# A linear-attention and bilinear-GLU block on one core: the last seven block products, six of them turned so that the weights stand still

## The chip, the cores and the metric

The kernel runs on one core of one Trainium2 chip. The core has a matrix engine (TensorE, PE in the profile), three engines for elementwise work (VectorE or DVE, ScalarE or ACT, GpSimd or POOL) and SyncE (SP), which here issues every transfer between the chip's memory (DRAM) and the on-chip buffers. A matmul holds one 128-wide operand still in the array (it is loaded first, "PEld" in the profile) and streams the other through it, up to 512 columns at a time, and adds the result into a bank of the accumulator memory (PSUM). The metric is the device time of one execution in microseconds (us), and a kernel's time is the median of its runs.

## What is computed

The reference is one transformer block with modulated layer norms: linear attention, then a bilinear gated feed-forward part. Only the second half matters here:

```python
h = _layernorm(x, axis=-1) * (1 + cb) + sb
# _B_ref:
g = jnp.einsum("bsd,df->bsf", x, w_gate)
u = jnp.einsum("bsd,df->bsf", x, w_up)
h = g * u
return jnp.einsum("bsf,fd->bsd", h, w_down)
# and the end:
x = x + gb * _B_ref(h, B_w_gate, B_w_up, B_w_down)
```

There are S = 2048 tokens, D = 512 model columns and F = 1376 hidden columns, all in 32-bit floats. The stage that is changed is the last einsum for the second 1024 tokens, and the addition to x behind it.

## The kernel before

**Numbers.** Every 32-bit matrix is split into a high and a low part (ACT rounds the high part, DVE or POOL subtracts it to get the low one), and a product of two matrices is three matmuls: high by high, high by low, low by high. The helper `split` (L198 to L200) and `h_split`, `h_next`, `w_split` of the class `Down` do this; their outputs are called kh and kl for the hidden values, w for the weights.

**Tokens and columns.** The tokens stand in four chunks of 512 (`NCH` = 4, `CH` = 512), a chunk in four tiles of 128 tokens by 512 columns (`xts[ch][j]`, j = 0 to 3). Token p*4 + j of a chunk stands in partition p of tile j (views `xv` and `ov`, L53). The hidden columns stand in eleven tiles of 128, the last with 96.

**Gate and up.** For two chunks at a time these products are done as 2x2 blocks with seven block products in place of eight (sums and differences of blocks are formed first; s1 to s4 on the left, t1 to t4 on the right). `block` (L1180) is one hidden tile's pass of seven products of 6 matmuls with 512 tokens moving; it has named points (p1, p5, p6, p2, p7, p3, p4) behind its products, at which other work is handed in. The table `plan`, filled by `Down.planned` (L1485) and by a literal at the end of the kernel, says what happens at which point of which block; this sets the order of each engine's work. All instructions of an engine run in the written order. All transfers stand in one queue on SP, and one that has to wait holds those behind it.

**Down.** For chunks 0 and 1 plain products (`down_group`, L1237) run between the blocks. For chunks 2 and 3 the class `Down` (L1352) again uses seven block products. With c0 = chunk 2 and c1 = chunk 3, `a11` and `a12` are chunk 2's hidden values of the first and second tile of a pair, `a21` and `a22` those of chunk 3; `b11`, `b12`, `b21`, `b22` are the two row tiles of w_down by its two halves of 256 columns (`HALF`). There are five pairs, and one odd tile of 96 rows. While the last blocks run, the weight sums are formed, split, stored to DRAM (`w_park`) and fetched back (`w_fetch`, L1399) shortly before their product.

**The last stage.** `Down.run` (L1519) starts when the last block is done. Its products, in order: p1 = a11 b11, p2 = a12 b21, p3 = s2 t2, p4 = s1 t1, p5 = s3 t3, p6 = s4 b22, p7 = a22 t4; p2, p5, p6 and p7 also carry the odd tile. Before, in all of them the hidden values of one 128-token tile stand still and the weights move. p1, p3, p5 and p7 use `mm` (L1452): 256 weight columns move, three matmuls for each pair and token tile, four token tiles in two banks (`C`, the first two of `others`). p1, p3, p5, p7 add up in the same banks, and after each of them DVE adds what stands there to the part of x to which it belongs. p2, p4 and p6 use `mm_wide` (L1462): high and low weights move together as 512 columns, then the low hidden values with 256; they have four banks of their own (`A`, the list `banks`). The function `add` (L1525) adds a bank's part to a half of x's columns and stores the tile when it is complete. So each part of x stays in place as tokens by columns, and only 12 stores leave, eight of 128 KB and four of 256 KB. The last product is done tile by tile, in the order 0, 2, 1, 3, each tile's addition and store behind it.

Of the kernel before, what the change touches and what calls it, by code (L numbers as in the profile page):

```python
# [8 lines left out]
F32 = mybir.dt.float32  # L9
# [5 lines left out]
P = 128  # L15
NB = 94
BL = 32
# [7 lines left out]
def tile_adaln_block(  # L25
# [27 lines left out]
    xv = x[0].rearrange("(c p j) d -> c j p d", p=P, j=NJ)  # L53
    ov = out[0].rearrange("(c p j) d -> c j p d", p=P, j=NJ)
# [61 lines left out]
    def load_x(ch):  # L116
        return [load(xv[ch, j], "x") for j in range(NJ)]
# [827 lines left out]
    def evac(ch, dn, js=range(NJ), last=False, cols=((0, D),)):  # L945
        for j in js:
            xt = xts[ch][j]
            for a, b in cols:
                nc.vector.tensor_tensor(xt[:, a:b], dn[j][:, a:b], xt[:, a:b], op=ALU.add)  # L949
                if last:  # L950
                    nc.sync.dma_start(ov[ch, j, :, a:b], xt[:, a:b])
# [342 lines left out]
    banks, others = [], []  # L1294
# [18 lines left out]
    def ffn():  # L1313

        m = 0
        for g, (cs, fs) in enumerate(groups):
# [19 lines left out]
        wide_down = Down((2, 3), m, draws.pop(m))  # L1336
        wide_down.planned()
# [14 lines left out]
    class Down:  # L1352

        def __init__(self, cs, m, odd):
            self.cs, self.m, self.odd = cs, m, odd
# [4 lines left out]
            self.raw, self.t = {}, {}  # L1360

        def w_split(self, key, src, low=None):
            n = src.shape[0]
            w = B("w", (P, 2, HALF), F32R)[:n]
            nc.scalar.activation(w[:, 0], src, AF.Copy)
            (low or nc.vector).tensor_tensor(w[:, 1], src, f32(w[:, 0]), op=ALU.subtract)
            self.w[key] = w

# [93 lines left out]
        def mm_wide(self, bs, j, pairs, start):  # L1462

            a, b = j * P, (j + 1) * P
            for (h, l), w in pairs:
                k = h.shape[0]
                nc.tensor.matmul(bs[j], h[:, a:b], w[:k].rearrange("p t c -> p (t c)"), start=start, stop=False, skip_group_check=True)  # L1467
                nc.tensor.matmul(bs[j][:, :HALF], l[:, a:b], w[:k, 0], start=False, stop=False, skip_group_check=True)
                start = False

        def product(self, bs, js, left, right, start, odd=None):
            pairs = [(self.parts[i][left, "split"], self.w[right, i]) for i in range(self.NI)]
            if odd:
                pairs.append((self.h[LATE[0]][odd[0]], self.w["odd", odd[1]]))
            for j in js:
                if len(bs) == NJ:
                    self.mm_wide(bs, j, pairs, start)
                else:
                    self.mm(bs, j, pairs, start and j % 2 == 0)
# [5 lines left out]
        def planned(self):  # L1485
# [3 lines left out]

            put(1, "p6", lambda: nc.vector.tensor_tensor(self.odd, self.odd, gb[:self.odd.shape[0]], op=ALU.mult))  # L1490
# [27 lines left out]

        def run(self):  # L1519

            c0, c1 = self.cs
            x = lambda c, half, j: xts[c][j][:, half * HALF:(half + 1) * HALF]
            A, C = banks, others[:2]

            def add(c, half, bs, js, store=None):  # L1525
                for j in js:
                    parts = [bs[j][:, :HALF], bs[j][:, HALF:]] if bs is A else [self.part(bs, j)]
                    for ps in parts:
                        nc.vector.tensor_tensor(x(c, half, j), x(c, half, j), ps, op=ALU.add)
                    if store:  # L1530
                        a, b = store
                        nc.sync.dma_start(ov[c, j, :, a:b], xts[c][j][:, a:b])

            lo, hi, js = (0, 1), (2, 3), range(NJ)
            pairs = range(self.NI)
            last = self.NI - 1
# [4 lines left out]
            self.product(C, js, "a11", "b11", True)  # L1541
            self.drop("a11", "b11")
            self.h_next("s2", 0, 1)
            add(c0, 0, C, js)
            self.w_fetch("t1")
            self.product(A, js, "a12", "b21", True, (0, 0))
            self.drop("a12", "b21")
            self.h_next("s2", 2, 3, 4)
            add(c0, 0, A, js)
            self.w_fetch("t3")  # L1550
            self.product(C, js, "s2", "t2", False)
            self.drop("s2", "t2")
            self.h_split("s1", *pairs)
            add(c0, 1, C, js)
            self.w_fetch("b22")
            self.product(A, js, "s1", "t1", True)
            self.drop("s1", "t1")
            self.h_split("s3", *pairs)
            self.h_next("s4", 0)
            add(c1, 1, A, js)  # L1560
            self.w_fetch("t4")
            self.product(C, js, "s3", "t3", False, (1, 1))
            self.drop("s3", "t3")
            self.h_next("s4", 1, 2, 3, 4)
            add(c1, 1, C, js, (HALF, D))
            self.product(A, js, "s4", "b22", False, (0, 1))
            self.drop("s4", "b22")
            self.h_split("a22", *pairs)
            add(c0, 1, A, js, (0, D))
            before = []  # L1570
            for j in (0, 2, 1, 3):
                self.product(C, (j,), "a22", "t4", False, (1, "turn"))
                add(c1, 0, C, before, (0, HALF))
                before = (j,)
            add(c1, 0, C, before, (0, HALF))
# [266 lines left out]
```

## Time and profile before

| | us |
|---|---|
| median of three runs (lowest, highest) | 539.75 (539.24, 540.11) |
| the profiled execution | 539.46 |
| its span, first to last instruction | 537.7 |
| matrix engine busy in the span | 531.5 |
| last stage, first product to the end of the last | 478.46 to 534.05 |
| store queue's last issue starts | 534.50 |

The page of a profile gives for each engine the busy time and its share of the span, and the chain of work that ended last, followed back from the last instruction to what released it. Rows of the chain and of the timeline begin with the start and the length in us; then come the engine, the line of the kernel, the operation, the names of the tiles (written tile, arrow, read tiles), the shape and the count; a bracket at the end gives the idle time before it and what ended it. "SPq" is the transfer queue of SP: its length is what an issue takes on SP, not the transfer itself. Rows of one line's instructions give shortest, median and longest duration in ns. Grouped lines end in total busy us, mean ns of one, and idle time before.

### The profile page before, as it was taken

The page shows a single profiled execution, that of the slowest core. Times are in us where ns is not written, and L with a number is a line of the kernel's source. Part 1 is how long each engine was busy: PE and PEld are TensorE (multiplying, and loading weights), DVE is VectorE, ACT ScalarE, POOL GpSimd, SP SyncE. Part 2 cuts the span into 40 slices and gives each one's busy share as a digit, 9 for nine tenths or more (in the row PEclk, how much of TensorE's full clock was granted, in tenths as well). Part 3 has the DMA queues.
Part 4 walks back from the last instruction along what each step waited for, and adds up shares of the span by engine and source line. Part 5 has one row for each costly group of instructions (what it writes and reads, how often), then busy time and mean ns, then how long its engine had stood idle before and what let it go on. Part 6 is the DMA issues. An engine that isn't in the chain of part 4 may idle for free.

```text
span 537.7 us, 8020 instructions
## 1 busy us (share of the span) xinstructions
PE 531.5 (99%) x2537; PEld 443.4 (82%) x2537; DVE 406.7 (76%) x698; ACT 301.9 (56%) x572; POOL 159.0 (30%) x169
## 2 busy tenths in 40 slices
PE   8999999999999999999999999999999999999997
PEld 6888888888788878878888888887888888889996
DVE  7997879999989888769765576996555564669771
ACT  3696878768587765577684545454434334246030
POOL 2001010000021220085796577747532313210000
PEclk9999999999999999999999999999999999999999
DMA  8912426320165165856869595794289998789122
GB/s 276 385 43 92 144 99 214 86 72 2 45 196 199 36 213 161 280 159 222 290 196 322 196 335 206 232 374 109 81 295 341 395 394 294 237 301 389 53 79 79
DMA packets 86682, 109.21 MB, mean 203 GB/s; under 512 B 11184, under 2 KB 41904, under 8 KB 86640
## 3 DMA queue, kind: packets, MB, share of 16 engines
q1 hardware_dynamic: 86640, 108.70, 60.0%
q8 instruction: 20, 0.33, 0.3%
q14 instruction: 22, 0.18, 0.1%
HBM read 65.93 MB, written 42.73 MB: 202 GB/s over the span
## 4 chain that ended last, share of the span: by engine, by line
PE 93%; DVE 4%; ACT 2%; issue 1%; ACTq 0%; DVEq 0%
PE bank L1162 27%; PE acc L879 8%; PE acc L1162 7%; PE acc L1459 6%; PE bank L214 3%; PE bank L212 3%; PE bank L213 3%; PE bank L1467 3%; PE acc L1246 3%; PE acc L1245 3%; PE acc L1247 3%; PE acc L421 2%; PE acc L420 2%; PE acc L419 2%; PE bank L962 2%; PE bank L964 2%
## 5 line engine op out<-in xcount | busy, mean ns | idle before, releaser
L1162 PE MATMUL bank<-h,w 128*128 128x512 f32 (+1 forms) x630 | 145.3, 389 | 0.0
L1162 PEld LDWEIGHTS bank<-h,w 128*128 128x128 f32 (+1 forms) x630 | 117.0, 186 | 25.9
L1167 ACT ACTIVATE bank<-bank 128x512 f32<-128x512 f32 (+1 forms) x30 | 17.5, 584 | 74.5 <-PE bank L1162 74.4
L200 DVE TENSOR_TENSOR kl<-u,kh 128x512 fp32r<-128x512 f32 (+1 forms) x38 | 26.8, 752 | 23.8 <-ACT kh L199 21.8
L268 POOL TENSOR_TENSOR rstd<-ve,half 128x2 f32<-128x2 f32 (+3 forms) x13 | 11.8, 910 | 107.7 <-DVE ve L267 64.3
L212 PE MATMUL bank<-w,h 128*128 128x512 f32 x104 | 40.6, 391 | 0.0
L214 PE MATMUL bank<-w,h 128*128 128x512 f32 x104 | 40.6, 390 | 0.0
L213 PE MATMUL bank<-w,h 128*128 128x512 f32 x104 | 40.5, 390 | 0.0
L1162 PE MATMUL acc<-h,w 128*128 128x512 f32 x168 | 38.7, 389 | 0.0
L200 POOL TENSOR_TENSOR w<-raw,w 128x512 fp32r<-128x512 f32 (+1 forms) x15 | 22.3, 1496 | 51.7 <-ACT w L199 46.5
L879 PE MATMUL acc<-w,xh 128*128 128x512 f32 x120 | 37.1, 390 | 0.5 <-ACT acc L870 0.5
L1162 PEld LDWEIGHTS acc<-h,w 128*128 128x128 f32 x168 | 31.5, 188 | 6.5
L1124 POOL TENSOR_TENSOR w<-raw,w 128x256 fp32r<-128x256 f32 (+3 forms) x22 | 24.4, 1107 | 37.6 <-ACT w L1117 33.4
L949 DVE TENSOR_TENSOR x<-acc,x 128x512 f32<-128x512 f32 x40 | 26.5, 686 | 11.5 <-PE acc L1247 11.0
L1459 PE MATMUL acc<-w,kh 128*128 128x256 f32 (+1 forms) x176 | 31.8, 283 | 0.0
L1124 POOL TENSOR_TENSOR w<-t,w 128x512 fp32r<-128x512 f32 (+1 forms) x22 | 29.7, 1352 | 0.0
L1459 PEld LDWEIGHTS acc<-w,kh 128*128 128x128 f32 (+1 forms) x176 | 27.5, 192 | 0.2
L879 PEld LDWEIGHTS acc<-w,xh 128*128 128x128 f32 x120 | 22.4, 188 | 5.4 <-ACT acc L870 0.8
L419 PE MATMUL acc<-kh,xh 128*128 128x512 f32 x64 | 25.1, 392 | 0.0
L421 PE MATMUL acc<-kl,xh 128*128 128x512 f32 x64 | 25.0, 390 | 0.0
L420 PE MATMUL acc<-kh,xl 128*128 128x512 f32 x64 | 24.9, 390 | 0.0
L1245 PE MATMUL acc<-w,kh 128*128 128x512 f32 x64 | 24.9, 389 | 0.0
(257 smaller groups left out, 1325.1 us busy)
## 6 DMA issues: line engine op xcount, KB each, us to landing
right<-w SPq DMA_DIRECT2D x56, 256.0 KB, 3.6
w<-right SPq DMA_DIRECT2D x56, 256.0 KB, 5.1
raw<-in_w_mod_dram SPq DMA_DIRECT2D x24, 256.0 KB, 4.3
raw<-in_B_w_down_dram SPq DMA_DIRECT2D x20, 256.0 KB, 4.1
down_t<-w SPq DMA_DIRECT2D x20, 256.0 KB, 5.1
w<-down_t SPq DMA_DIRECT2D x20, 256.0 KB, 5.4
x<-in_A_x_dram SPq DMA_DIRECT2D x16, 256.0 KB, 5.4
down_b<-w SPq DMA_DIRECT2D x15, 256.0 KB, 5.1
```

The lines of the kernel that those rows point to most:

```text
L200: (low or nc.vector).tensor_tensor(l, src, f32(h), op=ALU.subtract)
L212: nc.tensor.matmul(ps, ah, bh, start=i == 0, stop=False)
L213: nc.tensor.matmul(ps, ah, bl, start=False, stop=False)
L214: nc.tensor.matmul(ps, al, bh, start=False, stop=i == n - 1)
L419: nc.tensor.matmul(tacc[k], xh[:, a:b], kh, start=first, stop=False)
L420: nc.tensor.matmul(tacc[k], xl[:, a:b], kh, start=False, stop=False)
L421: nc.tensor.matmul(tacc[k], xh[:, a:b], kl, start=False, stop=last)
L879: nc.tensor.matmul(yps[i], x, y, start=False, stop=k == KD - 1 and x is al, skip_group_check=True)
L1124: sub = lambda out, x, y: (on or nc.gpsimd).tensor_tensor(out, x, f32(y), op=ALU.subtract)
L1162: mm = lambda x, y, **kw: nc.tensor.matmul(ps, x[:, k], y, skip_group_check=True, **kw)
L1245: nc.tensor.matmul(ps, hh[:, a:b], dh[:n, c:d], start=i == 0, stop=False)
L1459: nc.tensor.matmul(ps, x[:, a:b], y, start=start, stop=False, skip_group_check=True)
```

## The change

Six of the seven products are turned: 128 weight columns stand still and the 512 tokens of a whole chunk move. `turned` replaces `mm_wide`:

```diff
+        def turned(self, bank, left, right, fresh, odd=None):
+
+            for m in range(2):
+                ps, start = sets[m][bank], fresh
+                for (h, l), w in self.pairs(left, right, odd):
+                    k = h.shape[0]
+                    of = w[:k, :, m * P:(m + 1) * P]
+                    for x, y in ((0, h), (0, l), (1, h)):
+                        nc.tensor.matmul(ps, of[:, x], y, start=start, stop=False, skip_group_check=True)
+                        start = False
+            self.drop(left, right)
```

The 256 columns of a half go in two sets of 128: set 0 has the even columns, set 1 the odd ones. So that each set is contiguous, `w_split` writes the split weights in that order (all but t4 and the odd tile's difference, which p7 uses as before):

```diff
+            if key[0] != "t4" and key[1] != "turn":
+                src = src.rearrange("p (r m) -> p m r", m=2)
+                h, l = (x.rearrange("p (m r) -> p m r", m=2) for x in (h, l))
+            nc.scalar.activation(h, src, AF.Copy)
+            (low or nc.vector).tensor_tensor(l, src, f32(h), op=ALU.subtract)
```

All eight banks are used, four for each set (`sets`). Bank a holds p1 and then also p2; after p1 ACT copies a to b, to which p3 is added; after p3 ACT copies b to c, to which p5 is added; d holds p4, then p6 is added. So the result of these products stands as columns by tokens. It is copied to the on-chip buffers and brought back in 32x32 blocks by DVE (`flip`), which leaves blocks of 32 tokens by 64 columns; x is read a second time from a copy in DRAM in the same blocks (`x_rows`, written by `x_store` during four of the blocks, read by `x_blocks`), DVE adds it (`finish`), and the blocks go to the output as runs of 64 floats (`move`, four transfers of 64 KB for each tile of 128x512):

```diff
+        def blocks_of(self, rows, half, u):
+
+            cols = rows[u * HALF:(u + 1) * HALF, half * HALF:(half + 1) * HALF]
+            return cols.rearrange("(b i) (q f) -> q i b f", i=BL, q=NQ)
+
+        def move(self, t, of, out):
+            for q in range(NQ):
+                sb = t[q * BL:(q + 1) * BL].rearrange("i (b f) -> i b f", f=2 * BL)
+                nc.sync.dma_start(*((of[q], sb) if out else (sb, of[q])))
...
+        def flip(self, ys):
+
+            out = []
+            for u in range(2):
+                t = B("t")
+                for m in range(2):
+                    nc.vector.transpose(t.rearrange("p (b e m) -> p b e m", m=2, e=BL)[..., m],
+                                        ys[m][:, u * HALF:(u + 1) * HALF].rearrange("p (b i) -> p b i", i=BL))
+                out.append(t)
+            return out
+
+        def finish(self, ts, c, half):
+            rows = out[0][c * CH:(c + 1) * CH]
+            for u, (t, xb) in enumerate(zip(ts, self.xb.pop((c, half)))):
+                nc.vector.tensor_tensor(t, t, xb, op=ALU.add)
+                self.move(t, self.blocks_of(rows, half, u), True)
```

The block of chunk 3's first half, called c21, is the exception: p7 still makes its part as tokens by columns. What bank c holds for it is turned by `flip`, written to DRAM in runs of 64, read back as four tiles of tokens by columns, and added to x late, between p7's pieces. The core of `run`:

```diff
+            self.turned(a, "a11", "b11", True)
+            for m in both:
+                self.h_next("s2", m)
+                copy(sets[m][b], sets[m][a])
...
+            self.turned(a, "a12", "b21", False, (0, 0))
...
+            self.turned(c, "s3", "t3", False, (1, 1))
+            self.x_blocks(c1, 1)
+            self.x_blocks(c0, 1)
+            self.h_next("s4", 1, 2, 3, 4)
             self.h_split("a22", *pairs)
+            c11 = self.flip(c11)
+            u3 = self.flip(to_sbuf(c))
+            c21 = tc.dram_tile([CH, D], F32, name="c21")
+            for u, t in enumerate(u3):
+                self.move(t, self.blocks_of(c21, 0, u), True)
+            p5 = self.flip(onto(c, p5))
+            self.finish(c11, c0, 0)
+            u3 = [load(c21.rearrange("(j p) d -> j p d", p=P)[j][:, :HALF], "u") for j in js]
+            self.turned(d, "s4", "b22", False, (0, 1))
+            self.finish(p5, c1, 1)
+            u2 = self.flip(onto(d, u2))
+            self.finish(u2, c0, 1)
...
             for j in (0, 2, 1, 3):
+                self.product(C, (j,), "a22", "t4", (1, "turn"))
+                add(*before)
                 before = (j,)
+                if j == 1:
+                    for i in js:
+                        nc.vector.tensor_tensor(x(i), x(i), u3[i], op=ALU.add)
+                        if i % 2 == 0:
+                            nc.sync.dma_start(ov(c1, i)[:, :HALF], x(i))
+            add(*before)
```

For chunks 2 and 3 the token order becomes plain: tile j holds tokens j*128 to j*128 + 127 of the chunk (`tokens`). `planned` is called before the first block instead of after the eighth, so that the stores of x can be put into blocks 5 to 8.

**Where instructions move.** First the end of SP's queue. Before, its last rows are the twelve stores of x's tiles to the output:

```order
L1532 DMA out_dram<-x_156 128x256
L1532 DMA out_dram<-x_158 128x256
L1532 DMA out_dram<-x_160 128x256
L1532 DMA out_dram<-x_162 128x256
L1532 DMA out_dram<-x_148 128x512
L1532 DMA out_dram<-x_150 128x512
L1532 DMA out_dram<-x_152 128x512
L1532 DMA out_dram<-x_154 128x512
L1532 DMA out_dram<-x_156 128x256
L1532 DMA out_dram<-x_160 128x256
L1532 DMA out_dram<-x_158 128x256
L1532 DMA out_dram<-x_162 128x256
```

Now there stand (t_5710 and t_5713 are c21's blocks, t_5700 and t_5703 those of chunk 2's first half, t_5727 and t_5730 chunk 3's second, t_5799 and t_5802 chunk 2's second half; 32x8x64 is a transfer of 32 partitions with 8 runs of 64):

```order
L1550 DMA c_5716<-t_5710 32x8x64 x4
L1550 DMA c_5716<-t_5713 32x8x64 x4
L1550 DMA out_dram<-t_5700 32x8x64 x4
L1550 DMA out_dram<-t_5703 32x8x64 x4
L116 DMA u_5743<-c_5716 128x256
L116 DMA u_5745<-c_5716 128x256
L116 DMA u_5747<-c_5716 128x256
L116 DMA u_5749<-c_5716 128x256
L1550 DMA out_dram<-t_5727 32x8x64 x4
L1550 DMA out_dram<-t_5730 32x8x64 x4
L1550 DMA out_dram<-t_5799 32x8x64 x4
L1550 DMA out_dram<-t_5802 32x8x64 x4
```

Four plain stores of 128x256 follow. So 40 transfers stand where there were 12, and the last four are behind all the others. Ahead of these rows, among and behind the last weight loads, stand 24 more of 32x8x64, the loads of x.

Second, ACT around p1 and p2. Before (kh of s2, five pairs, then of s1):

```order
L1435 ACTIVATE kh_5393<-u_4333 128x512
L1435 ACTIVATE kh_5398<-u_4593 128x512
L1435 ACTIVATE kh_5465<-u_4779 128x512
L1435 ACTIVATE kh_5470<-u_4965 128x512
L1435 ACTIVATE kh_5475<-u_5151 128x512
```

Now, with acc_4549 and bank_2881 the two sets of bank a, acc_4550 and bank_2882 those of bank b:

```order
L1444 ACTIVATE kh_5373<-u_4343 128x512
L1170 ACTIVATE acc_4550<-acc_4549 128x512
L1444 ACTIVATE kh_5379<-u_4603 128x512
L1170 ACTIVATE bank_2882<-bank_2881 128x512
L1444 ACTIVATE kh_5431<-u_4789 128x512
L1444 ACTIVATE kh_5436<-u_4975 128x512
L1444 ACTIVATE kh_5441<-u_5161 128x512
```

The copies stand between the first splits; p2's first matmul writes acc_4549 and waits for the first copy.

Third, DVE behind the last subtractions for a22. Before, eight additions from p6's banks follow, then the four of p7:

```order
L200 TENSOR_TENSOR kl_5839<-u_5217,kh_5838 128x512
L1529 TENSOR_TENSOR x_148<-x_148,bank_2881 128x256 x2
L1529 TENSOR_TENSOR x_150<-x_150,bank_2882 128x256 x2
L1529 TENSOR_TENSOR x_152<-x_152,bank_2883 128x256 x2
L1529 TENSOR_TENSOR x_154<-x_154,bank_2884 128x256 x2
```

Now (u_5505 and u_5506 are bank a's copies, u_5706 and u_5707 bank c's):

```order
L203 TENSOR_TENSOR kl_5697<-u_5227,kh_5696 128x512
L1565 STREAM_TRANSPOSE t_5700<-u_5505 128x256
L1565 STREAM_TRANSPOSE t_5700<-u_5506 128x256
L1565 STREAM_TRANSPOSE t_5703<-u_5505 128x256
L1565 STREAM_TRANSPOSE t_5703<-u_5506 128x256
L1565 STREAM_TRANSPOSE t_5710<-u_5706 128x256
L1565 STREAM_TRANSPOSE t_5710<-u_5707 128x256
L1565 STREAM_TRANSPOSE t_5713<-u_5706 128x256
L1565 STREAM_TRANSPOSE t_5713<-u_5707 128x256
L1592 TENSOR_TENSOR u_5591<-acc_4551,u_5591 128x512
L1592 TENSOR_TENSOR u_5592<-bank_2883,u_5592 128x512
```

The transposes of c11 and c21 come directly behind the subtractions, and the additions of p4's copies to bank c behind them. The first tile of c21, with which SP's rows above begin, is complete with the sixth transpose.

More of the change, by code (lines that the diff above doesn't have):

```diff
@@ L1460, in mm, with pairs @@
                     start = False
[L1462 to L1471, printed above, removed]
+        def pairs(self, left, right, odd):
             pairs = [(self.parts[i][left, "split"], self.w[right, i]) for i in range(self.NI)]
@@ L1548, in run @@
             self.h_next("s2", 2, 3, 4)
-            add(c0, 0, A, js)
             self.w_fetch("t3")
-            self.product(C, js, "s2", "t2", False)
-            self.drop("s2", "t2")
+            self.turned(b, "s2", "t2", False)
             self.h_split("s1", *pairs)
-            add(c0, 1, C, js)
+            c11 = to_sbuf(a)
+            for m in both:
+                copy(sets[m][c], sets[m][b])
+            u2 = to_sbuf(b)
             self.w_fetch("b22")
-            self.product(A, js, "s1", "t1", True)
```

98 lines of the change are left out of this document (54 added, 44 removed).

## The prediction

> **What bounds the kernel now.** I read the page's busy table and chain first, then the last stage piece by piece, then the queue that carries the output.
>
> ```profile
> span 537.7 us, 8020 instructions
> ...
> PE 531.5 (99%) x2537; PEld 443.4 (82%) x2537; DVE 406.7 (76%) x698; ACT 301.9 (56%) x572; POOL 159.0 (30%) x169
> ...
> PE 93%; DVE 4%; ACT 2%; issue 1%; ACTq 0%; DVEq 0%
> ```
>
> PE is busy for 99% of the span and carries 93% of the chain that ended last, so a shorter PE shortens the kernel only as long as nothing else ends later. The stage that is edited, in the chain in order of time (start, length, what):
>
> ```profile
> 468.94 9.52 PE bank L1162 x42
> 478.46 7.19 PE acc L1459 x60
> 485.65 0.23 PE bank L1467
> ...
> 494.08 7.18 PE acc L1459 x60
> 501.26 0.23 PE bank L1467
> ...
> 508.33 8.63 PE acc L1459 x72
> 516.97 0.23 PE bank L1467
> ...
> 525.39 8.63 PE acc L1459 x72
> 534.05 0.42 DVE x L1529
> ```
>
> The seven products (p1 to p7 below) start at 478.46, 485.65, 494.08, 501.26, 508.33, 516.97 and 525.39, with no gap, and p7 ends at 534.05. Behind it stand one 0.42 us addition and one store. The store queue (SP) in the same stretch, then its issue durations (min/median/max in ns) and the time from issue to landing:
>
> ```profile
> 493.76 6.77 SPq L1404 DMA_DIRECT2D w<-down_t  x5
> 515.09 19.74 SPq L1532 DMA_DIRECT2D out_dram<-x  x12
> ...
> L1532 SPq DMA_DIRECT2D out_dram<-x x12: 332/332/359, 515.1 to 534.5; - x12
> ...
> DMA to landing us min/median/max: 1.9/2.2/3.8
> ```
>
> Twelve plain stores in 19.74 us at 0.33 us each: SP waits, it does not work. Its last issue starts at 534.50, 0.45 us behind PE's end, and 3.2 us later the span ends. The question is whether this stays so.
>
> **PE: what is saved.** A 512-wide matmul costs 9.52/42 = 0.2267 us (first row of the chain), a 256-wide one 7.19/60 = 0.120. Each of p1 to p6 becomes two sets of 15 (with the odd tile 18) matmuls of 512: 30 x 0.2267 = 6.80 us, or 36 x 0.2267 = 8.16. p1, p3 and p4 have 30, p2, p5 and p6 have 36: 3 x (6.80 + 8.16) = 44.9 us against 525.39 - 478.46 = 46.9. **Saved on PE: 2.0 us.** p7 stays as it is (8.66 us).
> The Trainium skill, page "TensorE: Matmul & The Clock Gate", section "Wait — 56ns, not 53.3ns?", gives a matmul N cycles at 2.4 GHz plus about 2.5 ns. By that a 512 would be 0.216 us and a 256 0.109, and the saving an estimated 0.3 us in place of 2.0. The rows above say 0.2267 and 0.120, some 10 to 13 ns a matmul, so this trace doesn't agree, and I go by the rows; by that page the first rival below would come out as no change.
>
> **PE: a wait that is new.** p2 now adds to the very bank that p1 has filled, after ACT has copied it to another. ACT's rows, with the copy's duration from the grouped lines:
>
> ```profile
> 484.38 1.23 ACT L1435 ACTIVATE kh<-u 128x512 fp32r<-128x512 f32 x2 [5.09 <-DVE u L1421]
> ...
> 490.76 2.70 ACT L199 ACTIVATE kh<-s 128x512 fp32r<-128x512 f32 x5
> ...
> L1167 ACT ACTIVATE bank<-bank 128x512 f32<-128x512 f32 x2 | 1.2, 582 | 2.7 <-PE bank L1162 2.7
> ```
>
> The copy stands behind the first split of s2 on ACT, which DVE lets start at 484.38: 484.38 + 0.62 + 0.58 = 485.6. p1 ends at 478.46 + 6.80 = 485.26. So PE waits 0.3 us, with all of its queue behind (none if ACT is earlier, 0.9 if both copies stood in front). The copy of the second set waits for p1's end and holds three splits of s2 behind it, which p3 needs only 8 us later. The other copies lie a whole product ahead of their use. The new times on PE: p2 485.6, p3 493.8, p4 500.6, p5 507.4, p6 515.5, p7 523.7, end 532.4, which is 1.65 us before 534.05.
>
> **DVE: when the first transposed block is ready.** The rows that price it:
>
> ```profile
> 501.97 3.10 DVE L200 TENSOR_TENSOR kl<-u,kh 128x512 fp32r<-128x512 f32 x5
> 507.03 3.23 DVE L1529 TENSOR_TENSOR x<-x,bank 128x256 f32<-128x256 f32 x8
> ...
> 291.75 1.29 DVE L341 STREAM_TRANSPOSE wide<-u 128x512 f32<-128x512 f32 x2
> ```
>
> One 128x512 operation is 0.60 us, one 128x256 (3.23/8, from PSUM) 0.40, and a 128x512 transpose 0.60 like the others; so a 128x256 transpose is taken at 0.33 (half and a little), bounded by 0.30 and 0.60, since its result is written to every second element, which no row here does. After p3's end at 500.6 ACT has three copies (3 x 0.58) and five splits of s3 (2.70): 505.1, and DVE's last subtraction 505.7. DVE then has 15 operations of 128x512 (five sums, ten subtractions for s4 and a22) = 9.0, and some 1.0 in which ACT makes the two copies of p4's result between the splits: 515.7. Four transposes of c11 and the first two of the block c21: 6 x 0.33 + 0.1 = 2.1. **The first new store can go at 517.8.** The old additions (0.40 each) are gone from DVE, and the 16 transposes, four 128x512 additions from PSUM, six of x and eight of 128x256 that replace them end, added up in this way, at about 527.5. PE's third piece of p7 waits for one of them, the addition of the first piece, and is due at 523.7 + 2 x 2.16 = 528.0; transposes at 0.60 would make PE wait some 4 us there.
>
> **SP: what the new stores cost.** The only rows with such a shape (64 KB in 128 runs, three dimensions on each side):
>
> ```profile
> 198.68 7.72 SPq L337 DMA_DIRECT2D u<-second  x16
> 269.29 8.87 SPq L1006 DMA_DIRECT2D stowed<-n  x16
> ...
> L1006 SPq DMA_DIRECT2D stowed<-n x32: 332/443/1668, 238.4 to 277.7; - x32
> L1006 SPq DMA_DIRECT2D stowed<-n x4: 391/443/1444, 241.2 to 242.7; - x4
> L337 SPq DMA_DIRECT2D u<-moved x56: 303/430/582, 144.9 to 237.8; - x56
> L337 SPq DMA_DIRECT2D u<-first x32: 319/430/775, 48.4 to 85.1; - x32
> L337 SPq DMA_DIRECT2D u<-second x16: 376/430/549, 198.7 to 206.0; - x16
> ```
>
> Loads: 7.72/16 = 0.48 us from issue to issue. Stores: 8.87, less the 1.2 by which the longest issue (1668) passes the median, over 16 = 0.48 again. Against 0.33 for a plain one that is the price of the third dimension. From 517.8 SP has to issue, in this order, 8 stores of c21, 8 of c11, four loads of c21, 8 of c22, 8 of c12, four plain stores: 32 x 0.48 = 15.4, four loads at 0.40 = 1.6, three plain ones ahead of the last at 0.36 = 1.1. The data is always there first (c11's first tile at about 521.6, when c21's stores are out; c12's second at 527, when the queue is at 533). **The last issue starts at 517.8 + 18.1 = 535.9, not at 532.9** (PE's end plus 0.45). That is 1.4 us behind the 534.50 of now: PE's 1.65 us are gone, SP is the last engine.
> To this I add the long issue: of the 32 stores two took 1.0 and 1.2 us more than the median (1444 and 1668), of the 104 loads none. Two in 136, with 36 such transfers: 36 x 2/136 x 1.1 = 0.6 us (none to 2.4). The sum is +1.4 + 0.6 = **+2.0 us**.
>
> **What costs nothing.** The 24 loads of x blocks (24 x 0.48 = 11.5) stand behind the weight loads that end at 500.5 and fit before 517.8; without that cover the final additions would be late by their sum. The four loads of c21 land at about 529, and the additions that need them are due before 532.4. For the rest four rows: SP among the blocks that store x, a block's busy time, the last weights and what such a load takes to land.
>
> ```profile
> 375.86 12.57 SPq L951 DMA_DIRECT2D out_dram<-x  x4
> 450.00:460.00 10.00, 10.00 (x46) 8.28 (x45) 5.05 (x8) 3.70 (x8) 2.14 (x3) 1.00 0.73 222
> 477.06 2.38 SPq L1404 DMA_DIRECT2D w<-down_b  x5
> ...
> w<-down_b SPq DMA_DIRECT2D x15, 256.0 KB, 4.6
> ```
>
> The eight stores of x (8 x 0.35) fall where SP spends 12.57 us on four issues. Splits that read every second element cost ACT and POOL between once and twice today's; in 10 us of the blocks these work 3.70 and 2.14. Even with the last splits 2 us later p2's five weights would land from 484 to 486.3; it needs them from 485.6 to 488.3. Tokens in another order move the same 2 KB rows.
>
> **DMA engines.** Two stretches, plain 2 KB rows and then runs of 512 B (length, busy time of PE, PEld, DVE, ACT, POOL, then clock, DMA share, GB/s):
>
> ```profile
> 431.00:434.00 3.00, 3.00 (x15) 2.49 (x14) 1.77 (x3) 0.96 (x2) 0.00 (x0) 1.00 1.05 402
> 270.50:277.50 7.00, 7.00 (x33) 5.79 (x32) 4.72 (x6) 6.39 (x13) 6.67 (x6) 1.00 0.49 118
> ```
>
> 402 GB/s are 196 packets of 2 KB in a us, so one costs 16 x 1.05/196 = 86 ns of an engine; 118 GB/s of 512 B are 230, so 34 ns. A run of 64 floats is 256 B: on the line through both 25 ns, flat 34 ns. A store has 256 runs: 0.41 to 0.54 us on 16 engines, against 0.48 of issue. I take the line (the size counts in the one pair of rows that I have), so issue decides.
>
> **The rivals.** *PE still ends last* (faster): if SP takes these stores at the plain price of 0.36, its last issue could start at 532.0, and the end follows PE's (532.9 in place of 534.5): -1.6 us, 537.9. For it speaks the 332 ns minimum of such a store; against it the median of 443. It turns at 0.39 us a store.
> *The queue at its bare price*: 0.43 a transfer without the gaps and no long issue, 1.6 less than the 15.4: -0.2, 539.3, no change. The loads' median of 430 speaks for it, their 7.72/16 against it.
> *The DMA engines decide*: flat 34 ns, 0.54 a store, 17.3 in place of 15.4: 1.9 more than +1.4, about +3.3, 542.8.
> *Short writes count double*: if HBM takes a run of 256 B by reading and writing it back, a packet costs twice 34 ns and a store 1.09 us: 32 x 1.09 = 35 in place of 15.4, with the 1.4 +21 us, 560. No row here is below 512 B on the way out, so nothing excludes it; that 512 B stay at 34 ns, near the line, speaks against a cliff right below. The Trainium skill, page "DMA: Bandwidth & Descriptors", section "Specifications", states that below 512 B the DMA engine reads, modifies and writes; by that rule this rival is the outcome, and no run here shows it.
>
> **How the numbers follow.** Everything is counted against the profiled execution, 539.46 us with its span of 537.7; the median of the three runs is 539.75, 0.3 more. Forecast, the SP queue ends last with +1 to +3 us: 0.43, at 539.46 + 2.0 = 541.5. PE still last 0.14, bare price 0.20, DMA engines 0.15, double writes 0.08. 0.2% (1.1 us) is what a measurement tells from no change: slower 0.43 + 0.15 + 0.08 = 0.66, same 0.20, faster 0.14. The range 538.3 to 544.5 leaves out the double writes and most of the first rival; the forecast's own is 540.5 to 542.5.
>
> **What would show it.** SP issuing without a gap from about 518 to the end, 40 transfers back to back, at 0.48 a piece; the chain of waits ending in SP and DMA, no longer in PE; PE's last matmul near 532.5 with six products of 6.8 or 8.2 us, and a wait of some 0.3 us at p2's start. If SP is idle between stores and waits for DVE, my DVE chain is wrong; if stores land later and later behind their issue (far over the 2 us of now), the DMA engines decide; if the last store starts within 0.5 us of PE's end, the forecast is wrong.

## The result, and the profile after

| | us |
|---|---|
| changed kernel, median of 6 runs (lowest, highest) | 543.88 (543.11, 544.61) |
| kernel before, beside it, median of 6 runs | 539.86 (539.18, 540.45) |
| ratio, 95% interval | 1.0075 (1.0065 to 1.0086) |
| the profiled execution of the changed kernel | 543.11, span 541.4 |

The changed kernel is 4.0 us slower; the forecast was 541.5, +2.0. The measured time lies inside the stated range of 538.3 to 544.5, and above the 540.5 to 542.5 of the forecast itself. First the page's busy table and its chain.

```profile
span 541.4 us, 7851 instructions
...
PE 530.1 (98%) x2407; PEld 437.0 (81%) x2407; DVE 405.3 (75%) x692; ACT 308.5 (57%) x584; POOL 157.4 (29%) x169
...
PE 90%; DVE 5%; ACT 3%; issue 1%; DVEq 0%; ACTq 0%
```

Read by itself, this page would say that nothing has changed: PE is busy for 98% and carries 90% of the chain. The end of the chain in order of time (start, length, what) shows why that is misleading.

```profile
485.32 0.49 ACT acc L1170
485.81 0.04 issue
485.86 4.41 PE acc L1489 x18
...
524.36 8.63 PE acc L1468 x72
533.00 0.02 issue
533.02 0.42 DVE x L1641
```

The chain ends at 533.4, the span at 541.4. The 8 us in between belong to no engine that counts as busy. They are found in SP's timeline (start, length, line, what, count) and in its issue durations (minimum/median/maximum in ns, first and last start):

```profile
518.20 3.86 SPq L1550 DMA_DIRECT2D c<-t  x8
522.16 3.94 SPq L1550 DMA_DIRECT2D out_dram<-t  x8
526.19 2.52 SPq L116 DMA_DIRECT2D u<-c  x4
528.80 7.97 SPq L1550 DMA_DIRECT2D out_dram<-t  x16
536.87 0.90 SPq L1654 DMA_DIRECT2D out_dram<-x  x2
537.86 0.88 SPq L1643 DMA_DIRECT2D out_dram<-x  x2
...
L1550 SPq DMA_DIRECT2D out_dram<-t x24: 382/456/472, 522.2 to 536.3; - x24
L116 SPq DMA_DIRECT2D u<-c x4: 382/398/1055, 526.2 to 528.3; - x4
L1643 SPq DMA_DIRECT2D out_dram<-x x2: 392/396/399, 537.9 to 538.3; - x2
```

Forty transfers back to back from 518.20 to the end, with no gap that could hold another issue. The last one starts at 538.3, 5.3 us behind PE's end; before it was 0.45 us. PE is 1.05 us earlier than before (533.00 against 534.05), and nobody benefits.

DVE in the same stretch, first what turns the blocks, then the last addition to a block and p7's additions:

```profile
516.10 2.73 DVE L1565 STREAM_TRANSPOSE t<-u 128x256 f32<-128x256 f32 x8
518.75 0.65 DVE L1592 TENSOR_TENSOR u<-acc,u 128x512 f32<-128x512 f32 x1
...
526.35 1.25 DVE L1573 TENSOR_TENSOR t<-t,x 128x512 f32<-128x512 f32 x2
527.51 0.41 DVE L1641 TENSOR_TENSOR x<-x,acc 128x256 f32<-128x256 f32 x1
```

The data of every new store is complete at 527.6, when SP has yet to issue 16 of them, from 528.80 on. Two windows of the stretch in which SP works that queue off (length, busy time of PE, PEld, DVE, ACT, POOL, then clock, DMA share, GB/s):

```profile
518.00:524.00 6.00, 6.00 (x28) 4.92 (x28) 6.00 (x14) 0.00 (x0) 0.00 (x0) 1.00 0.51 109
532.00:540.00 8.00, 0.98 (x9) 0.78 (x7) 0.42 (x1) 0.00 (x0) 0.00 (x0) 0.77 0.63 158
```

The DMA engines are busy for half to two thirds of the time. In the first window nearly all packets are runs of 256 B: 109 GB/s are 426 of them in a us, so one takes 16 x 0.51/426 = 19 ns of an engine.

### The profile page after: what moved, and what is told of

It is laid out like the page before. It is cut to its first block, busy times and chain, and to the rows that moved or that the text cites. A ratio compares the mean times of both kernels' runs of the same rounds, so it can differ in the third digit from the quotient of the medians.

```text
span 541.4 us, 7851 instructions
## 1 busy us (share of the span) xinstructions
PE 530.1 (98%) x2407; PEld 437.0 (81%) x2407; DVE 405.3 (75%) x692; ACT 308.5 (57%) x584; POOL 157.4 (29%) x169
## 4 chain that ended last, share of the span: by engine, by line
PE 90%; DVE 5%; ACT 3%; issue 1%; DVEq 0%; ACTq 0%
PE bank L1165 25%; PE acc L882 8%; PE acc L1165 7%; PE acc L1489 4%; PE bank L1489 4%; PE bank L216 3%; PE bank L217 3%; PE bank L215 3%; PE acc L1249 3%; PE acc L1250 3%; PE acc L1248 3%; PE acc L424 2%; PE acc L423 2%; PE acc L422 2%; PE bank L965 2%; PE bank L967 2%
## 5 line engine op out<-in xcount | busy, mean ns | idle before, releaser
L1170 ACT ACTIVATE bank<-bank 128x512 f32<-128x512 f32 (+1 forms) x32 | 18.7, 583 | 76.1 <-PE bank L1165 73.1
L1248 PE MATMUL acc<-w,kh 128*128 128x512 f32 x64 | 24.9, 389 | 0.0
L1250 PE MATMUL acc<-w,kl 128*128 128x512 f32 x64 | 24.9, 389 | 0.0
L1249 PE MATMUL acc<-w,kh 128*128 128x512 f32 x64 | 24.9, 389 | 0.0
```

Source lines behind the costliest of these rows:

```text
L1248: nc.tensor.matmul(ps, hh[:, a:b], dh[:n, c:d], start=i == 0, stop=False)
L1249: nc.tensor.matmul(ps, hh[:, a:b], dl[:n, c:d], start=False, stop=False)
L1250: nc.tensor.matmul(ps, hl[:, a:b], dh[:n, c:d], start=False, stop=i == len(hs) - 1)
```

## The experiments

Four theories stood at the start. **Q**: SP's issue of the new transfers decides, at about 0.50 us a piece. **D**: the DMA engines decide, through the short runs. **V**: DVE is late with the data. **W**: the total of the added work decides, wherever it stands. Each run was compared with the kernel before on the same chip (539.6 to 540.1 us there).

### Eight stores more

```diff
             self.finish(u2, c0, 1)
+            again = tc.dram_tile([CH, D], F32, name="again")
+            for u, t in enumerate(u2):
+                self.move(t, self.blocks_of(again, 1, u), True)
```

> c12's 8 block stores are issued a second time, into a scratch tensor. Q: 8 more issues of 0.50 us, +4.0 us, 547.9. D: 2048 more short runs at 25 to 34 ns on 16 engines, +3.2 to +4.4. V: no change, 543.9, since DVE does nothing more.

Measured: 548.19 (548.04 to 548.9), ratio 1.0149 (1.0134 to 1.0164), 4.3 us more than the changed kernel, 0.54 a transfer. The eight issues in SP's timeline:

```profile
537.40 4.01 SPq L1550 DMA_DIRECT2D again<-t  x8
```

They take 0.50 us each. Work at the tail of SP's queue comes through in full, and V, under which the tail has time to spare, falls. D does not: its +3.2 to +4.4 holds the 4.3 as well as Q's +4.0 does.

### Sixteen stores less

```diff
-            self.finish(p5, c1, 1)
+            for t, xb in zip(p5, self.xb.pop((c1, 1))):
+                nc.vector.tensor_tensor(t, t, xb, op=ALU.add)
...
-            self.finish(u2, c0, 1)
+            for t, xb in zip(u2, self.xb.pop((c0, 1))):
+                nc.vector.tensor_tensor(t, t, xb, op=ALU.add)
```

> The 16 block stores of c22 and c12 are left out (their additions are still done). Q: 16 x 0.50 = 8 us less on SP, of which 4.9 count, until PE's end decides again: 539.0. D: the same 539.0. V: 543.9, since DVE does what it did.

Measured: 538.55 (538.21 to 538.65), ratio 0.9967 (0.9954 to 0.9981). Sixteen issues at 0.50 would be 8.0 us, but only 5.3 come back, since PE then ends last again. This is the floor of the turned products in this form: 1.5 us under the kernel before on the same chip. So PE's saving is real.

### Two queues

```diff
-            self.finish(p5, c1, 1)
+            self.finish(p5, c1, 1, nc.scalar)
...
-            self.finish(u2, c0, 1)
+            self.finish(u2, c0, 1, nc.scalar)
```

(`finish` hands the engine on to `move`, which issues there.)

> The 16 block stores of c22 and c12 are issued by ACT instead of SP; nothing else changes. Theory Q (SP's issue of the stores, 0.50 us each, ends last): the last store starts 0.45 us behind PE's end again instead of 5.3 us behind it, so 543.9 - 4.9 = 539.0 us. Theory D (the DMA engines need their time for runs of 64, whoever issues them): 543 to 544, no gain. Theory V (DVE delivers the blocks too late): 543.9, no gain.

Measured: 542.0 (541.68 to 542.41), ratio 1.0034 (1.0022 to 1.0045): 1.9 us gained, where Q had 4.9. SP's and ACT's queues in this kernel, and two rows of the view of waits (who waited for whom: us, times, longest):

```profile
522.56 8.12 SPq L1550 DMA_DIRECT2D out_dram<-t  x8
530.79 1.91 SPq L116 DMA_DIRECT2D u<-c  x4
```

```profile
523.53 13.92 ACTq L1550 DMA_DIRECT2D out_dram<-t  x16
```

```profile
DVE x L1652 <- DMA u<-c: 4.7, 2, 4.2
...
SPq L1550 <- DMA out_dram<-t: 3.6, 2, 2.8
```

SP's eight stores of c11 take 8.12 us in place of 3.94, because SP now waits 3.6 us for transfers of stores (and one of the eight issues is a long one of 1.3 us, see below). So c21's loads go out at 530.79 in place of 526.19, and DVE waits 4.2 us for them. The program gives its transfers eight completion semaphores in turn, whichever queue issues them, so that a transfer waits for the one eight places before it. That this couples the two queues fits the rows, but was not tried by itself. The miss says nothing against Q: one wait was traded for another. And where both queues issue at the same time, their rows speak for it:

```profile
L1550 SPq DMA_DIRECT2D out_dram<-t x3: 452/458/482, 523.0 to 524.0; - x3
L1550 ACTq DMA_DIRECT2D out_dram<-t x3: 387/472/478, 523.5 to 524.5; - x3
```

Side by side, an issue still takes 0.39 to 0.48 us on each, so for about a microsecond twice as many transfers leave in the same time. There the pace is that of the engine that issues, and not of something behind both queues.

### Runs twice as long

Same number of transfers and bytes, each written as runs of 128 floats in place of 64, so with half the packets.

```diff
-                self.move(t, self.blocks_of(rows, half, u), True)
+                cols = rows[u * HALF:(u + 1) * HALF, half * HALF:(half + 1) * HALF]
+                of = cols.rearrange("(h b i) (g f) -> h g i b f", i=BL, h=2, g=2)
+                for q in range(NQ):
+                    sb = t[q * BL:(q + 1) * BL].rearrange("i (b f) -> i b f", f=4 * BL)
+                    nc.sync.dma_start(of[q // 2, q % 2], sb)
```

> The 24 block stores to the output keep their number, their bytes and their three dimensions, but have 128 runs of 128 floats in place of 256 runs of 64 (the blocks so land in other places of the output than the reference has them). Q: no change, 543.9 within 0.7. D: half the runs, so the stores stop deciding and the end falls back towards PE's, 539 to 541. V: no change.

Measured: 543.11 (542.64 to 543.67), ratio 1.0053 (1.0038 to 1.0068). 0.8 us gained, just over Q's margin and far from D's 3 to 5. Half the packets give each of 24 issues some 0.02 us (16 take 7.70 us from the first to the end of the last, against 7.97), which is 0.4 of the 0.8. D falls.

### Plain stores

```diff
-                self.move(t, self.blocks_of(rows, half, u), True)
+                plain = tc.dram_tile([P, D], F32, name=f"plain_{c}_{half}_{u}")
+                for q in range(NQ):
+                    nc.sync.dma_start(plain[q * BL:(q + 1) * BL], t[q * BL:(q + 1) * BL])
```

The 24 output stores keep their number and bytes, but each is 32 partitions of one 2 KB run, in two dimensions.

> The 24 block stores to the output go to scratch tensors instead, as 32 partitions with one run of 2 KB each (two dimensions); their number and bytes are the same, and these parts of the output are left unwritten. Price by shape: an issue falls from 0.50 to 0.36 us, 24 x 0.14 = 3.4, so 540.5. Price by transfer, whatever its shape: 543.9. Price by runs in the DMA engines (D): the stores stop deciding, 539.0.

Measured: 543.33 (542.94 to 543.43), ratio 1.0064 (1.005 to 1.0078). The issue durations, and SP's last sixteen stores:

```profile
L1576 SPq DMA_DIRECT2D plain<-t x24: 366/421/437, 522.0 to 536.3; - x24
...
529.34 7.39 SPq L1576 DMA_DIRECT2D plain<-t  x16
```

A plain store still takes 7.39/16 = 0.46 us where the strided one takes 0.50. So shape and runs together are worth 0.04 us. The remaining 0.46 belongs to the transfer as such.

### One store for four

```diff
-                for q in range(NQ):
-                    nc.sync.dma_start(plain[q * BL:(q + 1) * BL], t[q * BL:(q + 1) * BL])
+                nc.sync.dma_start(plain, t)
```

This starts from the plain stores: the last two runs kept number and bytes, so they could not tell a price per transfer from a price per byte.

> The changed kernel with each of the six finished output tiles of the part from DRAM written whole, as one transfer of 256 KB to a scratch area of the same size, in place of four transfers of 64 KB into the output (so those blocks of the output are not written). The bytes are the same, the transfers on SP are 18 fewer. P (SP pays per transfer, 0.49 us whatever it holds): SP runs out of work before p7 ends, its last issue follows PE's end again (533.0 + 0.45 in place of 538.3), 538.6 +- 0.7. B (the pace goes with the bytes, 64 KB in 0.49 us, because something behind the queue takes them at that rate): a transfer takes four times as long and nothing is gained, 543.6 +- 0.7.

Measured: 538.43 (538.03 to 538.82), ratio 0.9975 (0.9965 to 0.9986). SP and the end of the chain:

```profile
522.05 0.90 SPq L1575 DMA_DIRECT2D plain<-t  x2
...
525.01 3.82 SPq L1575 DMA_DIRECT2D plain<-t  x4
...
531.22 2.49 SPq L1644 DMA_DIRECT2D out_dram<-x  x2
```

```profile
532.93 0.42 DVE x L1642
```

The first two issues of 256 KB are 392 and 412 ns long, and the next transfer starts at 523.05, 0.50 us a piece, as with 64 KB. So 18 issues fewer bring 4.9 us, down to the floor of the sixteen stores less. SP's last issue follows PE's end once more. **The price is per transfer.** (Whether the true layout can be written with fewer transfers was not tried: this run leaves those blocks of the output unwritten.)

### The long issue

In the changed kernel one load of c21 holds SP for 1055 ns. Each of the six kernels above and of the two reordered ones below has one issue of 1.3 to 2.0 us on SP, which starts between 525 and 528. It isn't always the same transfer: in three of them it is a store. What they share is a packet in the DMA queue for instructions at about 526: here the changed kernel from 526 to 528 (queue: packets, MB, share).

```profile
q8 instruction: 1, 0.02, 2.9%
```

The page of the changed kernel counts 19 of them with 0.31 MB, 16 KB each. From the second on they come every 25 to 31 us, in which PE executes 229 to 285 instructions (matmuls and weight loads), so they look like the fetch of PE's code. If so, the fetch can be moved by adding instructions far ahead. The first attempt put 92 short matmuls in the place of 12 warm-up matmuls at the start:

```diff
-    keep_on(24)
+    keep_on(12)
+    for _ in range(92):
+        nc.tensor.matmul(ps_idle[:, :32], idle[:, :P], idle[:, :32], start=True, stop=True)
```

> The changed kernel with 12 of the 24 warm-up matmuls at the start replaced by 92 of 32 columns: 80 PE instructions more by count (160 with their weight loads) far ahead of the last stage, the same work otherwise. F (the one long issue of SP among the new stores is the moment at which 16 KB of instructions are fetched, every 256 instructions of PE): the fetch comes at about 509.5 in place of 526, no issue takes over 0.6 us between the first store of c21 and the last issue, and that stretch shrinks from 20.1 us to 19.0 (18.8 to 19.4); the time falls by 0.6 to 1.5 if the start is unchanged, 542.8. R (long issues fall at random or belong to the loads of c21): one of over 0.9 us is there again and the stretch stays at 20.1 +- 0.5, 543.8.

Measured: 559.28 (558.88 to 560.01), ratio 1.0361 (1.0345 to 1.0376). The start was spoilt: the warm-up ended at 23.5 us in place of about 10. Two windows of it (PE's matmuls stand behind its busy time, the granted clock behind POOL):

```profile
6.50:9.00 2.50, 2.50 (x24) 2.50 (x23) 2.24 (x9) 1.54 (x3) 1.09 (x2) 0.98 0.99 331
13.00:24.00 11.00, 11.00 (x54) 11.00 (x54) 0.77 (x2) 0.63 (x1) 0.00 (x0) 0.50 1.05 382
```

Each short matmul still loads 128x128 weights. At a granted clock of 0.98 one follows the other every 0.10 us (2.50/24). From about 9 us on the granted clock is 0.50, a load takes up to 0.34 us, and one matmul starts every 0.20 us (11.00/54). So it is not the loads alone that held the start up, as an expectation below has it: at 0.10 us the 92 would have taken some 9 us and not 17. Why the clock fell is not shown. The last stage shows the answer all the same: the stretch is 534.8 to 554.2, 19.4 us, with no issue over 0.48 us in it. The same edit in the reordered kernel below:

> The reordered kernel (the run with c11 added early, c22's stores ahead of c21's loads and ACT's copy ahead of the split), with the same 92 short warm-up matmuls in place of 12. F: the long issue among the loads of c21 (1.60 us) is gone, the last issue is 0.4 to 1.2 us earlier: 537.0 (536.4 to 537.6), since the fetch at 509.5 now lies among the loads of x blocks. R: 537.7 +- 0.6.

Measured: 553.23 (551.07 to 553.55), ratio 1.0236 (1.021 to 1.0262), spoilt in the same way (granted clock 0.50 from 12 to 24 us), and its time says nothing of the fetch. So once more with a cheap stationary operand:

```diff
-    keep_on(24)
+    for _ in range(88):
+        nc.tensor.matmul(ps_idle[:32, :32], idle[:, :32], idle[:, :32], start=True, stop=True)
+    keep_on(16)
```

> The changed kernel with 8 of the 24 warm-up matmuls replaced by 88 whose stationary operand has 32 columns as well as the moving one (in the first form the 92 weight loads of 128x128 cost 0.19 to 0.33 us each and held the start up to 23.5 us). F (long issue = code fetch): from the first store of c21 to the last issue 19.3 us (19.0 to 19.6) in place of 20.1, no issue over 0.6 us between them; 543.1 (542.6 to 543.5) if the start is not held up, and later by what p1's start is later than 478.8. R (the long issue is not the fetch): 20.1 +- 0.4 and 543.9.

Measured: 545.43 (544.68 to 545.95), ratio 1.0108 (1.0093 to 1.0124). The start is still held up, by 2.5 us (PE ends at 535.53). The rows of this kernel, the packets of 512 to 514 and then the issues:

```profile
q8 instruction: 1, 0.02, 3.0%
```

```profile
520.74 3.86 SPq L1552 DMA_DIRECT2D c<-t  x8
524.70 3.96 SPq L1552 DMA_DIRECT2D out_dram<-t  x8
528.76 1.84 SPq L116 DMA_DIRECT2D u<-c  x4
530.70 8.05 SPq L1552 DMA_DIRECT2D out_dram<-t  x16
...
L116 SPq DMA_DIRECT2D u<-c x4: 382/384/412, 528.8 to 530.2; - x4
L1645 SPq DMA_DIRECT2D out_dram<-x x2: 396/397/398, 539.8 to 540.3; - x2
```

The packet has moved to 512, the four loads take 1.84 us in place of 2.52, no issue is over 0.5 us, and the stretch from the first store to the last issue is 540.3 - 520.74 = 19.6 us in place of 20.1. At 513.4, where the packet now starts, SP has no issue to hold. The long issue goes where the fetch goes. Why a fetch holds SP's issue is not shown. Nor does the median prove it alone: 2.5 us of late start less 0.5 would be 545.9, and 545.43 was measured.

### c11 stored earlier

c11 is complete with p3, but the change turns and stores it behind c21. Here it is turned and added before the splits of s3, and its eight stores stand ahead of c21's:

```diff
+            c11 = self.flip(c11)
+            self.add_x(c11, c0, 0)
...
+            self.store(c11, c0, 0)
...
-            c11 = self.flip(c11)
...
-            self.finish(c11, c0, 0)
```

(`add_x` and `store` are the two halves of `finish`.)

> c11 is turned and added to x right after p3, where DVE has nothing to do, and its 8 stores stand in front of c21's on SP, where SP has nothing to do; all work stays. Theory Q (SP's issue behind the first store of c21 decides): 8 x 0.50 = 4.0 us less behind that point, of which some 0.5 are lost since c21's loads now wait for c21's stores to land: 540.4, within 0.7. Rival W (the end is set by work that the stores stand for, DVE's chain or the DMA engines' total load): 543 to 544, since nothing is taken away.

Measured: 539.68 (538.93 to 540.08), ratio 0.9996 (0.9987 to 1.0006). The same work with eight issues moved to where SP had waited brings 4.2 us; W falls. That is a little more than forecast for Q, and as fast as the kernel before. Not all of it is SP's own idle time put to use: with c11's transposes done earlier, DVE has c21's first tile ready 0.9 us sooner (SP's first store of c21 starts at 517.30 in place of 518.20).

### The order put right

On top of that, c22's stores go ahead of c21's loads, and ACT copies the first set for p2 ahead of the first split of s2:

```diff
-            for m in both:
-                self.h_next("s2", m)
-                copy(sets[m][b], sets[m][a])
+            copy(sets[0][b], sets[0][a])
+            self.h_next("s2", 0)
+            self.h_next("s2", 1)
+            copy(sets[1][b], sets[1][a])
```

> As e5, and c22's 8 stores stand in front of the four loads of c21, and ACT's first copy for p2 stands in front of the first split of s2. Q: SP's work behind 517.4 us is 24 stores x 0.50, four loads x 0.45 and three plain stores x 0.45 = 15.2, so its last issue starts at 532.6, about where PE's end (0.3 us earlier, since p2 no longer waits) puts it: 538.9, 1 us under the kernel before. W: 543.

Measured: 537.72 (537.41 to 539.18), ratio 0.9962 (0.9948 to 0.9977): **faster than both kernels**, 6.2 us under the changed one and 2.1 under the one before. The profiled execution is the slowest of the five (539.18); its queue and the end of its chain:

```profile
513.62 3.91 SPq L1550 DMA_DIRECT2D out_dram<-t  x8
517.64 3.95 SPq L1550 DMA_DIRECT2D c<-t  x8
521.69 3.94 SPq L1550 DMA_DIRECT2D out_dram<-t  x8
525.72 3.03 SPq L116 DMA_DIRECT2D u<-c  x4
528.85 3.95 SPq L1550 DMA_DIRECT2D out_dram<-t  x8
...
523.40 8.63 PE acc L1468 x72
532.03 0.02 issue
532.05 0.42 DVE x L1652
```

PE ends at 532.03, 0.97 earlier than in the changed kernel. Two thirds of this are the wait of p2 (0.34) and the slower first set of p2 behind it (4.41 us in place of 4.10); the rest is p1, which here begins 0.32 earlier (478.40 against 478.72). The two changes of this run were not tried one by one. SP's last issue starts at 534.4, so in this execution the queue, with one load of 1602 ns, is still 1.9 us longer than PE's work and one store. The other four executions, of which there is no profile, took 0.6 to 1.8 us less; in the three that took 1.5 to 1.8 less, most of that excess must be gone. The same kernel with the cheap warm-up:

> The reordered kernel with the same cheap warm-up. F: no long issue among c21's loads (1.60 us in the profiled run of the reordered kernel), so SP's last issue follows PE's end, 532.05 + 0.45: 537.1 (536.7 to 537.6), and less spread between runs than 537.4 to 539.2. R: 537.7 +- 0.6 with the same spread.

Measured: 540.47 (539.36 to 540.74), ratio 1.0011 (1.0001 to 1.002). PE starts this stage 3.1 us later (p1 at 481.54 in place of 478.40), so the kernel loses. Taken off, 540.47 - 3.1 = 537.3 agrees with F's 537.1, but 537.7 is within its margin too, and the spread of 1.4 us is not much less than 1.8. As a timing this run settles nothing. Its rows do say one thing: SP's last issue follows PE's end again, and no load of c21 takes over 0.44 us. The packet has moved to 512.7, and here SP is at work there, on the loads of x:

```profile
L1552 SPq DMA_DIRECT2D x<-x_rows x2: 449/880/1311, 512.6 to 513.1; - x2
```

One of them is now the long issue, with 1311 ns. In the two kernels with 92 short matmuls it is the same: a load of x of 1658 ns at 527.2 beside the packet of 527.3, and a store of 1069 ns at 526.5 beside the packet of 526.3.

## Why the prediction came out as it did

The mechanism was right: SP's queue ends last, PE's saving is lost behind it, the result is slower. The size was half of what came. By the terms of the sum, against the profiled executions:

- **PE's saving, 2.0 us.** The products p2 to p6 took 38.5 us (485.86 to 524.36), forecast 38.1; 0.31 of the difference lies in p2's first set, behind the wait (4.41 us, where the other sets of 18 take 4.10). And p2 began 0.26 later than forecast, because p1 did (478.72 against 478.46). So PE ended at 533.00, forecast 532.4. By the floor of the sixteen stores less the saving is worth 1.5 us.
- **The new wait at p2.** 0.3 us forecast; the copy ended at 485.81 against 485.6, and the view of waits gives 0.3. Right for the wait, though not for the slow set behind it. In the changed kernel both are hidden behind SP.
- **DVE.** First store 517.8 forecast, 518.20 measured (+0.4); additions done 527.5 forecast, 527.6 measured. The transposes that write every second element take 2.73/8 = 0.34 us, near the lower bound, so PE's third piece didn't wait.
- **SP, 32 stores at 0.48.** They took 16.06 us, 0.50 each (+0.7). The number was close, but the reason beside it was wrong: "the price of the third dimension". The plain stores refute it, and the row that would have told it is the first store of a burst against the ones behind it, in the changed kernel from 518.4 on:

```profile
L1550 SPq DMA_DIRECT2D c<-t x1: 303/303/303, 518.2 to 518.2; - x1
...
L1550 SPq DMA_DIRECT2D c<-t x2: 451/460/470, 518.5 to 519.0; - x2
```

  The same shape takes 303 ns when SP has been idle and 450 to 470 right behind another. The 332 ns of the twelve plain stores before were isolated ones; the same shape back to back takes 0.39 to 0.40. The prediction even shows the row against its own reason: five plain weight loads back to back, with no third dimension, at 477.06, take 2.38/5 = 0.48 us each. The Trainium skill, page "Perfetto Trace Analysis", section "DMA Instruction — HWDGE (DVE, Sync)", counts into the profiled time of an issue its wait for the shared descriptor generator. These rows would fit that, but no run took the generator by itself, and SP and ACT side by side, in the run with two queues, show no wait of one on the other. What the 0.45 us consist of stays open.
- **Loads and plain stores, 0.40 and 0.36.** The four loads took 2.61 us in place of 1.6 (+1.0, of which 0.65 is the long issue); three plain stores 1.43 in place of 1.1 (+0.35). This is the step that failed: the price of an isolated issue was put to issues in a full queue, and no row of the prediction has 0.40 or 0.36 for such a one.
- **The long issue, 0.6 by chance.** The size was met by luck (0.65 in the profile), the reason was wrong. It is not chance: one falls into this stretch in each of the nine kernels that leave the warm-up alone. The two long issues of the prediction's own rows, 1444 and 1668 ns, also stand in windows with an instruction packet.

Together: +0.4 + 0.7 + 1.0 + 0.35 = 2.4 behind the 535.9 of the sum, which is the 538.3 of the profile; the forecast had 0.6 of it.

Of the rivals, "PE still ends last" came out only where issues were taken away or moved. The bare price of 0.43 is excluded by all 32 stores. "The DMA engines decide" gave 542.8, nearer to 543.88 than the forecast, and is still wrong: a packet took 19 ns, not 34, the engines were a third to a half idle, and half the packets brought 0.8 us. **Short writes that count double** are refuted for this kernel: 68 ns a packet was that rival's price. The Trainium skill, page "DMA: Bandwidth & Descriptors", section "Specifications", has a read and a write back below 512 B; at 256 B no such cost shows here in the time.

One sign failed: the chain of waits was to end in SP and DMA. It still ends in PE: the page follows its chain back from the last addition, at 533.02, and nothing that it counts waits for the stores issued behind that.

## What to carry to other kernels

Count transfers, not bytes, where many stand in one queue at the end: here each held SP for 0.46 to 0.50 us, whether it moved 64 or 256 KB, and four in place of one cost the whole gain. Take the price of an issue from rows in which the queue is full, and look for idle time earlier in the queue: the same stores, issued as soon as their data was there, and one copy moved ahead on ACT turned +4.0 us into -2.1. A chain that ends well before the span is the sign to look at the queues.

## What the hardware showed that was not expected

- Back-to-back issues on SP cost 0.46 to 0.50 us nearly regardless of shape: 256 KB in one run a partition 0.50, 64 KB plain 0.46, 64 KB in runs of 512 B 0.48, in runs of 256 B 0.50; one after idle time 0.30 to 0.33. ACT, issuing beside SP for about a microsecond, took 0.39 to 0.48 and did not slow it.
- A packet of 256 B took about 19 ns of a DMA engine, less than the 25 to 34 worked out from runs of 512 B.
- SP's issue was held for 1.1 to 2.0 us when instructions were fetched, and the long issue left the stretch when the fetch did.
- Matmuls of 32 moving columns, each behind a 128x128 weight load, started every 0.10 us at a granted clock of 0.98 and every 0.20 us at 0.50. With 92 of them in the warm-up the clock was at 0.50 from about 9 us until they ended at 23.5; with 88 whose weights had 32 columns it stayed at 1.00.
